# Attention weights divided before they are spread, a residual on TensorE, the first norm on two engines, and one rank per step

## The chip, the core and the metric

The kernel runs on one core of one Trainium2 chip. The core has a matrix engine (TensorE, PE in the profile; its weight loads are the row PEld), a vector engine (VectorE, DVE), a scalar engine (ScalarE, ACT), GpSimd (POOL) and SyncE (SP), which here only issues transfers. Each works through its own list of instructions in order, and waits on semaphores for the others. Matmul results go to eight PSUM banks of 128 x 512 fp32; everything else lies in SBUF. The metric is the device time of one launch in microseconds (us): less is better.

## What is computed

One transformer block over 2048 positions of width 512, in bf16: x plus local attention of the normalised x, then that plus a gated MLP of its normalised self. Attention has 32 heads of 16; each position attends to 8 earlier ones, 0, 2, ..., 14 back.

```python
def _A_ref(x, wqkv, wo):                     # H = 32, Dh = 16, W = 8, dil = 2
    qkv = (x @ wqkv).reshape(B, S, 3, H, Dh).transpose(2, 0, 3, 1, 4)
    q, k, v = qkv[0], qkv[1], qkv[2]
    ...
    logits = jnp.einsum("bhsd,bhswd->bhsw", q, kg) * scale
    logits = jnp.where(mask[None, None, :, :], logits, -1e9)
    attn = _softmax(logits, axis=-1)
    o = jnp.einsum("bhsw,bhswd->bhsd", attn, vg)
    return o.transpose(0, 2, 1, 3).reshape(B, S, D) @ wo

def _B_ref(x, W_gate, W_up, W_down):         # W_gate, W_up: 512 x 1376
    gate, up = x @ W_gate, x @ W_up
    gate = gate * (gate > 0)
    return (gate * up) @ W_down

h = x + _A_ref(_layernorm(x), A_wqkv, A_wo)
return h + _B_ref(_layernorm(h), B_W_gate, B_W_up, B_W_down)
```

## The kernel before

The positions are cut into four chunks of 512, each into four blocks of 128 rows. The x rows stay in SBUF as `x_sm` and are overwritten by h. Each chunk goes through the same stages:

- First norm (`layernorm` without a residual): mean and variance of a block on DVE (L429, L432), 1/sqrt as Ln and Exp on ACT (L442, L446), the normalised rows (L487 on DVE for chunk 0, L484 on ACT for the others), four PE transposes of a block against the identity (L494), and a copy of two blocks at once out of PSUM (L512 on ACT; L510 on DVE for the second pair of chunk 0).
- q, k and v, transposed: twelve groups of four matmuls (L544), each copied out of PSUM by ACT (L552). In chunk 0 the first two groups are made in two halves of 256 positions.
- Scores: DVE multiplies q with four shifted views of k at once (L591, 128 x 4096; four of them in a chunk), PE sums over the 16 dimensions of a head with the 0/1 matrix `sel` (L597), ACT takes the exponential (L606). Chunk 0 multiplies the first 16 columns with a mask (L609).
- Spreading: each weight is copied over the 16 dimensions of its head by the 0/1 matrix `spread` (L625), and ACT copies the eight results to SBUF (L632). The sums of the weights come from the same matrix (L639); ACT makes 1/sum as exp(-ln) (L642, L645).
- Values: DVE multiplies the spread weights with eight shifted views of v (L662, four in a chunk), adds the eight in three steps (L665), and multiplies the result by 1/sum (L669).
- Output: four groups of four matmuls (L700); DVE adds x and takes the row sum at the same time (L705).
- Second norm: a small DVE step for the mean (L414), squares with a sum on ACT (L420), Ln and Exp (L439, L446), rows on DVE (L487), transposes and copies as above.
- MLP: 11 tiles of up and gate, 8 matmuls each (L727), copied by ACT (L731, and L734 with Relu), multiplied by DVE (L747); then for each block 11 matmuls (L759), an addition of h on DVE (L763) and a store from SP (L766).

The order is not the order of the loops. `add` records each step with an engine, an estimated length, what it depends on, and the buffers that it takes and uses. `Plan.order` then runs a list schedule: among the steps of an engine that could start within a small window (`LOOK`) of the earliest, it takes the one with the smallest `prio`, and gives it buffers from small pools: eight PSUM banks for all uses, five big buffers of 128 x 4096, three for exponentials, one for 1/sum. The order found is the order in which instructions are issued. `prio` comes from the table `PRIO`, one number for each kind of step and chunk, shared by all steps of that kind.

`setup` comes before all: it issues the loads (two for the x rows of chunk 0, one on SP and one on ACT), loads the ACT table, makes the constant matrices, and 54 small matmuls keep PE busy until the first rows are ready (`NWARM`, L522).

Of the kernel before, what the change touches and what calls it, by code (L numbers as in the profile page):

```python
# [8 lines left out]
P = 128  # L9
# [8 lines left out]
PRIO = {  # L18
    "warm": (329, 0, 0, 0),
    "xst": (-357, -495, 2394, -54),  # L20
    "xag": (-520, -862, -182, 1996),
    "xrl": (-362, -296, 194, 2166),
    "xre": (-82, 283, 2306, 886),
    "xxn": (-286, 2378, 367, 2013),
    "xtp": (540, 1594, 641, 716),
    "xte": (-646, 2834, 2727, 2443),
    "qkh0": (442, 0, 0, 0),
    "qkv0": (418, 417, 1697, 353),
    "qe0": (1262, 2340, 2135, 2291),
    "qkh1": (1644, 0, 0, 0),  # L30
    "qkv1": (449, 1372, 2578, 2742),
    "qe1": (2915, 2429, 2602, -366),
    "qkv2": (352, 2556, 1012, 1671),
    "qe2": (2725, 402, 863, 106),
    "qkv3": (453, 1501, 226, 815),
    "qe3": (2462, 2595, 2528, 2174),
    "qkv4": (1443, 695, 1687, 267),
    "qe4": (-122, 2839, 177, 2325),
    "qkv5": (701, 873, 594, 1878),
    "qe5": (-44, -211, -170, 2493),  # L40
    "qkv6": (862, 1457, 638, 395),
    "qe6": (-199, -327, 2260, -230),
    "qkv7": (487, 427, 68, 358),
    "qe7": (402, 2319, 2485, -311),
    "qkv8": (1720, 1667, 1519, 453),
    "qe8": (2802, 2488, 2656, 114),
    "qkv9": (1851, -242, 2722, 391),
    "qe9": (1309, 2749, 876, 2302),
    "qkv10": (1764, 857, 1851, 1678),
    "qe10": (2412, 1400, 2395, 458),  # L50
    "qkv11": (2427, 1522, 1794, 722),
    "qe11": (2598, 2825, -204, 2326),
    "pr0": (-482, 1697, -427, 2119),
    "sc0": (1698, 2659, 1551, 1498),
    "ex0": (2396, 2052, 1825, -25),
    "mk0": (2108, 0, 0, 0),
    "pr1": (-469, 1768, -500, 2606),
    "sc1": (404, 855, 418, 1193),
    "ex1": (1517, 142, -363, 143),
    "mk1": (-591, 0, 0, 0),  # L60
    "bc0": (1924, 469, 3082, 309),
    "be0": (-60, -227, 44, 2335),
    "bc1": (-281, 491, 1693, 187),
    "be1": (-373, 324, 2173, 119),
    "den": (1891, 635, 1806, 811),
    "dl": (2476, 2727, -37, 2595),
    "dr": (2494, 2236, 2409, 3002),
    "mu0": (-490, -741, -300, -559),
    "tree0": (-169, -269, -240, -508),
    "om0": (1670, 1359, 1810, -68),  # L70
    "mu1": (-422, -682, -366, -477),
    "tree1": (-140, -329, -243, -384),
    "om1": (-229, -267, 2395, -350),
    "mu2": (-555, -491, 2098, -268),
    "tree2": (-170, 1809, -660, 904),
    "om2": (-521, 1855, -320, -517),
    "mu3": (-551, 1681, 1796, 1815),
    "tree3": (-437, 1819, -540, 1964),
    "om3": (1672, 1855, -287, 2080),
    "wo0": (627, 1946, 489, 2577),  # L80
    "rs0": (-246, -458, -830, -312),
    "wo1": (438, 583, 385, 3140),
    "rs1": (-643, 2078, 1855, 2067),
    "wo2": (313, 69, 182, 553),
    "rs2": (-732, -369, -32, 1663),
    "wo3": (1166, 959, 49, 924),
    "rs3": (-414, -240, 1839, -148),
    "hnm": (-209, -423, 2603, -326),
    "hsq": (2388, 2706, 2324, -39),
    "hrl": (-604, -445, 2636, -334),  # L90
    "hre": (2395, -231, 2261, 2466),
    "hxn": (-412, -519, -293, -471),
    "htp": (609, 1635, 1868, 152),
    "hte": (1320, 2163, 155, 494),
    "mm0": (1484, 427, 528, 389),
    "ue0": (-673, 2837, 2251, 2336),
    "ge0": (44, 2326, -675, 97),
    "gu0": (2058, -433, -474, -124),
    "mm1": (823, 1820, 930, -289),
    "ue1": (1892, 191, 2067, -310),  # L100
    "ge1": (2639, 225, 2423, 2049),
    "gu1": (-496, -252, 1690, -742),
    "mm2": (-16, 412, 2609, 908),
    "ue2": (2776, 2713, -363, 2679),
    "ge2": (-65, 2678, 2266, 2262),
    "gu2": (2019, -373, -285, 1530),
    "mm3": (1801, -279, -278, 2624),
    "ue3": (2151, 164, 2100, 2147),
    "ge3": (-79, 2604, 224, -393),
    "gu3": (-491, -577, -568, 1516),  # L110
    "mm4": (471, 1194, -255, 2655),
    "ue4": (109, 43, 210, 2788),
    "ge4": (2240, 2269, 103, 3043),
    "gu4": (-304, -564, 2366, -656),
    "mm5": (88, 1884, 2524, 706),
    "ue5": (121, -114, 1286, 1403),
    "ge5": (-228, 2600, -52, 2852),
    "gu5": (-362, -366, 1055, 1556),
    "dn0": (415, 2726, 1868, 1679),
    "o0": (-185, 2463, -169, 1484),  # L120
    "os0": (-1500, -1424, -1612, -1426),
    "dn1": (438, 584, 2860, -448),
    "o1": (-495, -599, 1809, 1682),
    "os1": (-1609, -1383, -1616, -1425),
    "dn2": (1621, 2632, 1892, 368),
    "o2": (1891, -170, 2256, 1030),
    "os2": (-1268, -1189, -1208, -1424),
    "dn3": (2453, 2779, 469, 3112),
    "o3": (2772, 2257, -622, -485),
    "os3": (-1239, -1323, -1444, -1438),  # L130
    "xnb": (0, -605, -729, -589),
}
# [35 lines left out]
class Plan:  # L168
# [9 lines left out]
    def add(self, key, *a, **k):  # L178
        op = Op(*a, **k)
        op.key = key  # L180
        if key and key[0] in PRIO:
            op.prio = PRIO[key[0]][key[1]]
        op.seq = len(self.ops)
        self.ops.append(op)
        for b in set(op.take) | set(op.use):
            b.left += 1
        return op
# [57 lines left out]
def kernel(  # L245
# [18 lines left out]
    W = 8  # L264
# [26 lines left out]
    spread = sb.tile([P, P], BF16, name="spread")  # L291
    mask = sb.tile([P, 2, PADL], BF16, name="mask")
# [37 lines left out]
    sel_i, sp_i, mk_i = ints[:, 0:H], ints[:, H:H + P], ints[:, H + P:H + P + PADL]  # L330

    def setup():

        w3_r = A_wqkv.rearrange("(dt p) f -> p dt f", p=P)
        nc.sync.dma_start(x_sm[:, 0:2, :], x_rows[:, 0:2, :])
        nc.scalar.dma_start(x_sm[:, 2:4, :], x_rows[:, 2:4, :])
        for c, q in enumerate((nc.sync, nc.scalar, nc.sync)):
            q.dma_start(w3_sb[c][:], w3_r[:, :, c * D:(c + 1) * D])
        nc.sync.dma_start(x_sm[:, BPC:2 * BPC, :], x_rows[:, BPC:2 * BPC, :])
# [4 lines left out]
        for tk in range(2, NCK):  # L344
            nc.sync.dma_start(x_sm[:, tk * BPC:(tk + 1) * BPC, :], x_rows[:, tk * BPC:(tk + 1) * BPC, :])
# [11 lines left out]
        nc.gpsimd.iota(sp_i[:], pattern=[[1, H], [0, DQ]], base=0, channel_multiplier=0)  # L357
        nc.gpsimd.iota(mk_i[:], pattern=[[1, PADL]], base=0, channel_multiplier=0)
# [10 lines left out]
        V.tensor_scalar(out=spread[:], in0=sp_i[:], scalar1=cf[:, 1:2], scalar2=None, op0=ALU.is_equal)  # L369
        for hf in range(2):  # L370
            V.tensor_scalar(out=mask[:, hf, :], in0=mk_i[:], scalar1=cf[:, 2 + hf:3 + hf],
                            scalar2=None, op0=ALU.is_ge)
# [7 lines left out]
    NWARM = 54  # L380
    DMAT = ()

# [11 lines left out]
    xload = [None] * NCK  # L394
    for tk in range(NCK):
        xload[tk] = add(None, "LD", 0.0, None, lat=[3.3, 11.0, 22.0, 24.0][tk])
    wload = {n: add(None, "LD", 0.0, None, lat=v) for n, v in
             (("q", 5.7), ("k", 7.0), ("v", 8.5), ("o", 12.5), ("u", 16.5), ("g", 20.5), ("d", 28.0))}

    def layernorm(tk, src, dst_slots, pr, groups, on_act, residual=None):  # L400
# [7 lines left out]
        for grp in groups:  # L408
            ag, xns = [], {}
            lo, hi = grp[0], grp[-1] + 1  # L410
            for j in grp:
                if residual:
# [6 lines left out]
                    def f_sq(j=j, xn=xns[j]):  # L419
                        nc.scalar.activation(out=xn.t[:], in_=x_sm[:, tk * BPC + j, :], func=ACT.Square,  # L420
                                             bias=mv.t[:, j, 0:1], scale=1.0, accum_out=sq.t[:, j:j + 1])

                    a = add((ln + "nm", tk), "DVE", DSM, f_nm, [src[j]], pr, take=[mv], use=[sm], lat=DL)
                    ag.append(add((ln + "sq", tk), "ACT", AX + 0.2, f_sq, [a], pr, take=[sq, xns[j]], use=[mv], lat=AL))
                else:
# [8 lines left out]
                    a = add((ln + "st", tk), "DVE", DST, f_st, [src[j]], pr, take=[st], lat=DL)  # L434
                    ag.append(add((ln + "ag", tk), "DVE", DSM, f_ag, [a], pr, take=[mv], use=[st], lat=DL))

            def f_ln(lo=lo, hi=hi):
# [3 lines left out]
                else:  # L441
                    nc.scalar.activation(out=rs.t[:, lo:hi], in_=mv.t[:, lo:hi, 1], func=ACT.Ln,  # L442
                                         bias=eps_t[:, 0:1], scale=1.0)
# [10 lines left out]
            l = add((ln + "rl", tk), "ACT", AS, f_ln, ag, pr, take=[rs], use=[sq or mv], lat=AL)  # L454
            e = add((ln + "re", tk), "ACT", AS, f_ex, [l], pr, use=[rs], lat=AL)
            if on_act:
                e = add((ln + "nb", tk), "DVE", DSM, f_nb, [e], pr, take=[nb], use=[mv, rs], lat=DL)
# [69 lines left out]
    for tk in range(NCK):  # L527
# [49 lines left out]
        for hf in range(2):  # L577
# [38 lines left out]
            exd.append(a)  # L616


        ab, abd = Buf(big_s), []
        for hf in range(2):  # L620
            bcs = [Buf(at_s) for _ in range(4)]

# [195 lines left out]
```

## Time and profile before

| what | value |
|---|---|
| median of 8 runs | 211.1 us (211.01 to 212.92) |
| the profiled execution: its time, its span | 211.13 us, 209.3 us |
| PE busy, matmuls | 198.0 us (95%), 1122 |
| DVE busy, instructions | 169.4 us (81%), 253 |
| ACT busy, instructions | 137.7 us (66%), 262 |
| first q matmul | 9.54 us |
| first gate/up matmul | 74.31 us |
| last matmul ends | 205.89 us |
| chain of waits, by engine | PE 69%, DVE 24%, issue 3%, ACT 2%, DMA 2% |
| granted TensorE clock | 0.997 |

The span is what the profiler saw of the core, from the first to the last instruction; the time of a run is longer by what lies around it. The chain of waits is followed back from the last instruction: at each step to what released it, or to the instruction before it on its engine. In rows of the timeline the brackets give the idle time of the engine ahead of a group and what ended it.

### The profile page before, as it was taken

How to read it: one execution, taken by the hardware profiler on the slowest of the kernel's cores; microseconds unless marked ns; L12 is line 12 of the kernel's file. 1: busy time of each engine (PE TensorE's matmuls, PEld its weight loads, DVE VectorE, ACT ScalarE, POOL GpSimd, SP SyncE). 2: the span in 40 equal slices, each digit the busy share in tenths (PEclk: the TensorE clock that was granted, in tenths of full speed). 3: DMA queues.
4: the chain of work that ended last, by engine and by line, in shares of the span. 5: the costliest groups of instructions: out<-in, count | busy, mean ns of one | idle time of the engine just before them, and what ended most of it. 6: DMA issues, size and time to landing. Idle time of an engine off the chain costs nothing.

```text
span 209.3 us, 2967 instructions
## 1 busy us (share of the span) xinstructions
PE 198.0 (95%) x1122; PEld 96.7 (46%) x1142; DVE 169.4 (81%) x253; ACT 137.7 (66%) x262; POOL 1.6 (1%) x13
## 2 busy tenths in 40 slices
PE   8799899999998789999999999999999999999993
PEld 8664345544543344444454444444444445444441
DVE  5799999999998999999999999859999972122024
ACT  2369999979798887449776643677654644666210
POOL 3000000000000000000000000000000000000000
PEclk9999999999999999999999999999999999999998
DMA  6999800000000000000000000000000002000003
GB/s 203 366 401 375 266 7 2 0 0 0 3 0 0 0 3 0 0 0 3 0 27 25 0 30 0 8 17 28 0 25 0 25 28 75 0 0 2 3 21 105
DMA packets 8638, 10.71 MB, mean 51 GB/s; under 512 B 464, under 2 KB 7472, under 8 KB 8624
## 3 DMA queue, kind: packets, MB, share of 16 engines
q1 hardware_dynamic: 7824, 9.73, 13.4%
q10 hardware_dynamic: 800, 0.79, 1.1%
q8 instruction: 9, 0.15, 0.3%
q14 instruction: 5, 0.04, 0.1%
HBM read 8.42 MB, written 2.10 MB: 50 GB/s over the span
## 4 chain that ended last, share of the span: by engine, by line
PE 69%; DVE 24%; issue 3%; ACT 2%; DMA 2%; DVEq 0%; ACTq 0%
PE bank L727 36%; PE bank L759 18%; DVE big L591 8%; PE bank L700 5%; PE bank L544 5%; DVE big L665 4%; DVE big L662 4%; DVE st L429 3%; PE bank L494 2%; PE bank L597 2%; DMA x_sm<-in_A_x_dram 2%; DVE x_sm L705 1%; ACT quad L512 1%; DVE row L487 1%; DVE mv L432 1%
## 5 line engine op out<-in xcount | busy, mean ns | idle before, releaser
L727 PE MATMUL bank<-quad,wu_sb 128*128 128x512 bf16 (+1 forms) x173 | 44.9, 379 | 0.2
L727 PE MATMUL bank<-quad,wg_sb 128*128 128x512 bf16 (+1 forms) x173 | 44.7, 379 | 0.1
L759 PE MATMUL bank<-wd_sb,gT 128*128 128x512 bf16 (+1 forms) x170 | 39.7, 379 | 0.4 <-issue 0.2
L731 ACT CAST up_sb<-bank 128x512 bf16<-128x512 f32 (+1 forms) x44 | 25.6, 586 | 18.8 <-PE bank L727 12.2
L665 DVE TENSOR_TENSOR big<-big 128x2048 bf16<-128x2048 bf16 (+2 forms) x48 | 37.0, 777 | 1.0
L734 ACT ACTIVATE gr<-bank 128x512 bf16<-128x512 f32 (+1 forms) x44 | 26.1, 600 | 16.0 <-PE bank L727 13.1
L591 DVE TENSOR_TENSOR big<-quad,kT 128x4096 bf16<-128x4096 bf16 x16 | 36.0, 2284 | 0.7 <-ACT kT L552 0.7
L662 DVE TENSOR_TENSOR big<-big,vT 128x4096 bf16<-128x4096 bf16 x16 | 36.3, 2284 | 0.0
L747 DVE TENSOR_TENSOR gT<-gr,up_sb 128x1024 bf16<-128x1024 bf16 (+1 forms) x24 | 15.2, 641 | 25.6 <-ACT gr L734 25.4
L727 PEld LDWEIGHTS <-wu_sb 128*128 128x128 bf16 (+1 forms) x176 | 17.5, 100 | 20.8 <-issue 0.8
L727 PEld LDWEIGHTS <-wg_sb 128*128 128x128 bf16 (+1 forms) x176 | 17.6, 100 | 20.4
L759 PEld LDWEIGHTS <-gT 128*128 128x128 bf16 (+1 forms) x176 | 16.7, 98 | 20.2 <-issue 1.3
L632 ACT CAST big<-bank 128x512 bf16<-128x512 f32 x32 | 16.6, 627 | 2.3 <-PE bank L625 2.3
L512 ACT COPY quad<-bank 128x1024 bf16<-128x1024 bf16 x15 | 14.8, 1033 | 5.0 <-PE bank L494 5.0
L544 PE MATMUL bank<-quad,wv_sb 128*128 128x512 bf16 x61 | 15.7, 380 | 1.1 <-ACT quad L512 0.8
L544 PE MATMUL bank<-quad,wq_sb 128*128 128x512 bf16 (+1 forms) x65 | 15.5, 366 | 0.8 <-ACT quad L512 0.6
L544 PE MATMUL bank<-quad,wk_sb 128*128 128x512 bf16 (+1 forms) x67 | 15.5, 367 | 0.1
L420 ACT ACTIVATE row<-x_sm,mv 128x512 bf16<-128x512 bf16 x16 | 11.5, 733 | 5.3 <-DVE mv L414 5.3
L700 PE MATMUL bank<-wo_sb,quad 128*128 128x512 bf16 x63 | 14.6, 379 | 0.4 <-DVE quad L669 0.4
L763 DVE TENSOR_TENSOR row<-x_sm,bank 128x512 bf16<-128x512 bf16 x16 | 10.8, 684 | 4.7 <-PE bank L759 3.2
L429 DVE BATCH_NORM_STATS2 st<-x_sm 128x6 f32<-128x512 bf16 x16 | 10.5, 670 | 1.9 <-DMA x_sm<-in_A_x_dram 1.9
L597 PE MATMUL bank<-big,sel 128*32 128x512 bf16 x128 | 9.7, 384 | 2.5 <-DVE big L591 2.5
(55 smaller groups left out, 158.5 us busy)
## 6 DMA issues: line engine op xcount, KB each, us to landing
out_dram<-row SPq DMA_DIRECT2D x16, 128.0 KB, 1.7
x_sm<-in_A_x_dram SPq DMA_DIRECT2D x3, 512.0 KB, 15.1
wu_sb<-in_B_W_up_dram SPq DMA_DIRECT2D x1, 1376.0 KB, 13.2
wg_sb<-in_B_W_gate_dram SPq DMA_DIRECT2D x1, 1376.0 KB, 15.9
wd_sb<-in_B_W_down_dram SPq DMA_DIRECT2D x1, 1280.0 KB, 17.4
wq_sb<-in_A_wqkv_dram SPq DMA_DIRECT2D x1, 512.0 KB, 6.3
wk_sb<-in_A_wqkv_dram ACTq DMA_DIRECT2D x1, 512.0 KB, 7.0
wv_sb<-in_A_wqkv_dram SPq DMA_DIRECT2D x1, 512.0 KB, 7.5
```

What stands on the lines that cost most here:

```text
L429: V.bn_stats(out=st.t[:], in_=x_sm[:, tk * BPC + j, :])
L512: nc.scalar.copy(out=o, in_=i)
L544: nc.tensor.matmul(mm.t[:, lo:hi], lhsT=w3_sb[c][:, dt, t:D:NT], rhs=xnT.t[:, dt, lo:hi], start=(dt == 0), stop=(dt == NT - 1))
L591: V.tensor_tensor(out=pb.t[:].rearrange("p (t w) s -> p t w s", t=2), in0=q4, in1=k4, op=ALU.mult)
L632: nc.scalar.copy(out=ab.t[:, w, :], in_=bc.t[:])
L662: V.tensor_tensor(out=mt.t[:], in0=ab.t[:], in1=v8, op=ALU.mult)
L665: V.tensor_tensor(out=mt.t[:, 0:n, :], in0=mt.t[:, 0:n, :], in1=mt.t[:, n:2 * n, :], op=ALU.add)
L700: nc.tensor.matmul(od.t[:], lhsT=OT.t[:, t, j * P:(j + 1) * P], rhs=wo_sb[:, t, :], start=(t == 0), stop=(t == NT - 1))
L727: nc.tensor.matmul(mm.t[:fs, :], lhsT=w_sb[:, dt, ft * P: ft * P + fs], rhs=hnT.t[:, dt, :], start=(dt == 0), stop=(dt == NT - 1))
L731: nc.scalar.copy(out=ub.t[:fs, i, :], in_=um.t[:fs, :])
L734: nc.scalar.activation(out=gr.t[:fs, i, :], in_=gm.t[:fs, :], func=ACT.Relu)
L759: nc.tensor.matmul(od.t[:], lhsT=gts[ft].t[:fs, ft % 2, j * P:(j + 1) * P], rhs=wd_sb[:fs, ft, :], start=(ft == 0), stop=(ft == NFT - 1))
```

## The change

Six edits, of which the last replaces the whole table of priorities.

1. In chunks 1 to 3 (`EARLY`) the exponentials are multiplied by 1/sum before they are spread: two multiplications of 128 x 512 on DVE (`am0`, `am1`) instead of four after the sums of the values (`om`). A new 0/1 matrix `same` gives the sum of the weights in the layout of the exponentials. The last of the three additions writes the attention output directly.
2. In chunk 0 (`RPE`) the residual is a fifth matmul into the bank of the output group, against the identity. ACT copies the bank to `x_sm` and takes the row sum, and the squares of the second norm are taken from the bank.
3. The rows of chunk 0 are loaded block by block, two on SP and two on ACT. Blocks 0 and 1 are one group of the norm, block 2 and block 3 one each; the statistics of block 3 are two passes on ACT. Each block is copied out of PSUM by itself, blocks 1 and 3 by DVE. Four groups of q and k, not two, are made in halves.
4. The x rows of chunks 2 and 3 are loaded ahead of the weights of the output and of the MLP.
5. The last block of chunk 3 is finished in two halves of 256 columns: matmuls, addition, store.
6. `PRIO` gives way to `RANK`, 753 numbers, one for each call of `add`. Some estimated lengths and landing times change, and `NWARM` goes from 54 to 48.

`OPE` and `MERGE` are empty and `BCN` is 4, so the branches that they guard make no change.

```diff
+RANK = [
+    4, 1, 5, 2, 0, 3, 47, 6, 7, 29, 171, 229, 201, 272, 727, 10, 12, 8, 11, 14,
...
-        if key and key[0] in PRIO:
-            op.prio = PRIO[key[0]][key[1]]
+        if RANK:
+            op.prio = RANK[op.seq]
...
-        nc.sync.dma_start(x_sm[:, 0:2, :], x_rows[:, 0:2, :])
-        nc.scalar.dma_start(x_sm[:, 2:4, :], x_rows[:, 2:4, :])
+        for j in range(BPC):
+            (nc.scalar if j % 2 else nc.sync).dma_start(x_sm[:, j:j + 1, :], x_rows[:, j:j + 1, :])
...
-        nc.sync.dma_start(x_sm[:, BPC:2 * BPC, :], x_rows[:, BPC:2 * BPC, :])
+        for tk in range(1, NCK):
+            nc.sync.dma_start(x_sm[:, tk * BPC:(tk + 1) * BPC, :], x_rows[:, tk * BPC:(tk + 1) * BPC, :])
...
+        nc.gpsimd.iota(sm_i, pattern=[[0, 4], [1, H]], base=0, channel_multiplier=0)
+        V.tensor_scalar(out=same[:], in0=sm_i, scalar1=cf[:, 1:2], scalar2=None, op0=ALU.is_equal)
...
-    NWARM = 54
+    NWARM = 48
+    EARLY = (1, 2, 3)
+    RPE, OPE = (0,), ()
...
+                elif tk == 0 and j == BPC - 1:
+                    def f_su(j=j, xn=xns[j], sm=sm):
+                        nc.scalar.activation(out=xn.t[:], in_=x_sm[:, j, :], func=ACT.Copy,
+                                             accum_out=sm.t[:, j:j + 1])
...
+                        nc.scalar.activation(out=xn.t[:], in_=x_sm[:, j, :], func=ACT.Square,
+                                             bias=mv.t[:, j, 0:1], scale=-1.0, accum_out=mv.t[:, j, 1:2])
...
-        groups = [[0, 1], [2, 3]] if tk == 0 else [[0, 1, 2, 3]]
+        groups = [[0, 1], [2], [3]] if tk == 0 else [[0, 1, 2, 3]]
...
-                nc.tensor.matmul(dn.t[:], lhsT=spread[:], rhs=exs[hf].t[:], start=(hf == 0), stop=(hf == 1))
+                nc.tensor.matmul(dn.t[:], lhsT=(same if tk in EARLY else spread)[:], rhs=exs[hf].t[:], start=(hf == 0), stop=(hf == 1))
...
+        if tk in EARLY:
+            for hf in range(2):
+                def f_am(ex=exs[hf], rc=rc):
+                    V.tensor_tensor(out=ex.t[:], in0=ex.t[:], in1=rc.t[:], op=ALU.mult)
+
+                exd[hf] = add(("am%d" % hf, tk), "DVE", D2, f_am, [rcd], apr + 1, use=[exs[hf], rc], lat=DL)
...
+            if tk not in EARLY:
+                oev[t] = add(("om%d" % t, tk), "DVE", D2, f_om, [m, rcd], tpr, take=[OT], use=[mt, rc], lat=DL)
...
+                if tk in RPE:
+                    nc.tensor.matmul(od.t[:], lhsT=identity[:], rhs=x_sm[:, tk * BPC + j, :],
+                                     start=False, stop=True)
...
+                if tk in RPE:
+                    nc.scalar.activation(out=r, in_=od.t[:], func=ACT.Copy, accum_out=sm.t[:, j:j + 1])
...
+        parts = [(j, 0, D) for j in range(BPC)]
+        if tk == NCK - 1:
+            parts[-1:] = [(BPC - 1, 0, D // 2), (BPC - 1, D // 2, D)]
+        for n, (j, c0, c1) in enumerate(parts):
...
```

## The prediction

> **What bounds it now.** I read the time in slices first, then the chain of waits, then the order of instructions around the place where the chain changes engine.
>
> ```profile
> PE   8799899999998789999999999999999999999993
> DVE  5799999999998999999999999859999972122024
> ```
>
> Each digit is a fortieth of the span, 5.2 us. TensorE (PE) is full almost everywhere; VectorE (DVE) is equally full until four fifths of the span. Which of them sets the pace is told by the chain:
>
> ```profile
> 51.33 2.43 DVE x_sm L705 x8
> 53.76 0.25 DVE mv L414 x4
> 54.01 5.80 DVE big L591 x3
> ...
> 70.13 1.37 DVE row L487 x4
> 71.51 2.21 DVE big L591
> 73.72 0.04 issue
> 73.76 0.61 PE bank L597 x8
> 74.38 0.32 PE bank L727
> ```
>
> Columns are start, length, what. From 23 to 74 us the chain runs almost wholly through DVE; from 74 to 206 us through PE. At 70.13 DVE writes the normalised rows of chunk 0 (L487), and only then can the first gate/up matmul (L727) go. The busy times of the two stretches and of the worst part:
>
> ```profile
> 9.54:74.31 64.77, 59.93 (x402) 29.95 (x408) 62.24 (x80) 56.99 (x110) 0.00 (x0) 1.00 0.26 91
> 74.31:205.90 131.59, 130.78 (x655) 60.10 (x664) 100.12 (x150) 77.38 (x148) 0.00 (x0) 1.00 0.04 14
> ...
> 50.00:74.31 24.31, 21.45 (x165) 9.36 (x165) 23.60 (x26) 20.98 (x43) 0.00 (x0) 1.00 0.00 1
> ```
>
> After length come PE, weight loads, DVE, ACT. After 74.31 PE never stops (the missing 0.8 us are gaps of one matmul between unbroken neighbours). Before, PE loses 4.8 us, 2.9 of them after 50 us, when the q/k/v matmuls run out and DVE still works.
>
> Is a busy PE working at its rate? The Trainium skill warns ("Trainium Kernel Development and Optimization", Best Practices) that matmul busy time is a bad measure of the distance to the roofline. By that rule the 131 us could hide slack. The rows decide: groups of four L727 matmuls start at 109.23, 110.09 and 110.95, 0.216 us per matmul. The page "TensorE: Matmul & The Clock Gate" (Wait — 56ns, not 53.3ns?) gives 215.7 ns for 512 columns warm. The 131 us are work and move only by matmuls added or taken away. **So the end = first L727 start + about 131.6 + tail,** and the change is worth what it does to the start and the tail.
>
> **The parts.** All sums stand against the profiled execution: span 209.3, its own time 211.13, so 1.83 lies around the span; the median of the runs is 211.1, the same.
>
> *Head.* x comes in four loads, not two; three row blocks get their statistics on DVE, the fourth on ACT. Before:
>
> ```profile
> 7.28 1.42 DVE L487 TENSOR_SCALAR row<-x_sm,mv,rs 128x512 bf16<-128x512 bf16 x4
> 9.54 0.60 PE L544 MATMUL bank<-quad,wq_sb 128*128 128x256 bf16 x4 [0.38 <-ACT quad L512]
> ```
>
> Four statistics at 0.80 us each (4.07 to 7.28) precede the rows; then a 1024-wide copy of 1.02 us stands before q. Now three statistics end at 6.5, but xn waits for ACT: sum 0.72 and its read 0.19 (rows of L420), a small DVE step 0.15, square 0.72 and read, and the Ln/Exp of blocks 0 and 1 around it: about 7.0. Rows 0.34 each, transposes 0.35, 512-wide copies 0.6 by L731; the block-1 copy stands behind the other rows on DVE, until 9.05. First q matmul at about 9.1: -0.45. Bounds -0.8 (x lands earlier) and +0.2 (the fourth block lands last). The page "DMA: Bandwidth & Descriptors" (Anatomy of one DMA) prices a transfer at 2.0 us plus bytes/436 GB/s, fitted on another queue: halving 256 KB would save 0.3. The row is 3.3 us with other loads in flight, so I book 0. wq and wk are issued some 0.5 us later (two more issues, 0.43 to 0.51 each): landing 7.5 becomes 8.0, 8.3 becomes 8.8, still before use. x of chunks 2 and 3 now goes ahead of wo, up and gate weights: 1 MB, 2.6 us at 400 GB/s; wo is used at 48.9, the others at 74. The extra matrix `same` costs POOL 0.49 and DVE 0.28 (L357, L369) inside the DVE wait ending at 4.07. Six fewer warm-up matmuls shorten work that ends 0.88 before anything is ready: nothing.
>
> *Residual of chunk 0.* Four identity matmuls: +0.87 on PE. DVE loses 2.43 (the x8 row above); ACT gains four copies with a sum. By the page "ScalarE: Activation LUTs" (What ACT_TABLE_LOAD costs), 186 ns + 0.833 per element less 93 overlap gives 0.52 each, 2.1; it prices no sum. The nearest row, L420 with its sum, is 0.72, so up to 2.9. Either is more than DVE paid; it pays only because ACT is idle 3.3 us in the 24.3 above. I take 2.5.
>
> *Weights divided first.* In chunks 1 to 3 four multiplications per chunk (L669, 0.34 apart) become two. DVE: -4.1 + 2.0 = -2.1 over all. In exchange the spreading (L625) waits for sum 0.5, Ln 0.62, Exp 0.65, two multiplications 0.76 and hops: 2.7 us more latency per chunk. That hides behind other DVE work if the order leaves room. In the rank table the divisions of chunk 1 stand four large operations ahead of its first use in L662; those of chunks 2 and 3 lie among gate/up steps. Behind a late spread, PE holds score and q/k/v matmuls and ACT its copies L632, for which L662 on DVE waits. Exposed cost: 0, bound 2.7 for chunk 1 alone, since later PE has gate/up work.
>
> *Order.* Assigning the ranks to steps in the order of their `add` calls, DVE has 13 products L591 ahead of the normalised rows of chunk 0, not 12, and two divisions. Up to their end at 71.50: -2.43 (residual), +2.20 (product), +0.7 (divisions), -0.4 (statistics queued in fours, 0.69 a block where singles take 0.80; bounds 0 and -0.8), -0.7 (the wait for a key copy before 67.92: the keys of chunk 3 are ranked earlier; bounds 0 and -1.1). Sum -0.6: end at 70.9, bounds 70.1 and 72.0. From there 1.85 (71.50 to 73.35: transposes and copy) to the first L727: **72.8**, not 74.3. Could PE follow? Its work to that point: 59.9 + 0.87 + 0.55 (one score group more) - 0.33 (one spread less) = 61.0, from 9.1: 70.1 to 70.5 with small gaps. So PE still waits for DVE, 2.3 us.
>
> *Behind 72.8.* 131.6 - 0.55 + 0.33 = 131.4. DVE had 91.6 us from 71.5 to its last chunk-3 sum at 163.1; less 2.7 and one product less it ends near 157.6, well before PE needs it: no new stop. PE ends at 204.2.
>
> *Tail.* Now 3.4 us from the last matmul: L763 0.69, then the store. The last block is cut in halves: the half addition should take 0.36 (0.61 pitch, mostly per element); the half store saves 0.15 by the DMA page's rate, nothing if 1.7 is all latency. Tail 3.0, bounds 2.9 and 3.4. Twice as many weight loads (98 ns) still fit beside 256-column matmuls (0.109).
>
> Span 207.2; with 1.83: **209.0 us**, 1.0% less.
>
> **Rivals.** (a) *PE becomes the bound:* the DVE waits fall away and L727 starts at 70.5. 70.5 + 131.4 + 2.9 = 204.8, time 206.6. For it: DVE has 3 us of slack in its bounds; against it: a thirteenth product stands ahead. (b) *Nothing arrives:* the moved product and a remaining key wait eat the gain; L727 at 74.3, 205.7 + 3.0 = 208.7, time 210.5. For it: DVE's sum without the two estimates is +0.5. (c) *Slower: DVE waits in order for ACT.* The small residual steps (L414) and the chunk-1 division stand in DVE's queue ahead of three products and wait for ACT, which must first copy four residual blocks. DVE has three products, 6.6 us, to cover output matmuls 2.2, ACT copies and Exp 2.8: 5.0. The margin is 1.6. ACT was busy 23.7 of 25 us just before (25 to 50), and the four residual banks stay held until they are squared, so half of PSUM is gone while q/k/v still need copying. Once ACT is more than 1.6 late each us goes to the chain; 4 us gives L727 at 76.8, span 211.2, time 213.0.
>
> **Chances.** Forecast 0.45 (208.2 to 210.0), (a) 0.18, (b) 0.21, (c) 0.16. No change that can be told is within 0.5%, 210.0 to 212.2. Faster: forecast, (a) and a part 0.08 of (b), 0.71; same 0.13; slower 0.16. The range 206.7 to 212.0 leaves 0.06 below and 0.13 above.
>
> **What would show it.** Right: first q matmul near 9.1; L487 of chunk 0 ending near 71; first L727 near 72.8; PE unbroken after it; tail 3.0. Wrong: a DVE wait on ACT between 50 and 70 us, PE waiting for PSUM banks there, or a PE gap after 75 us because a spread came late.

## The result, and the profile after

The changed kernel takes 209.4 us (median; 207.58 to 209.87), the kernel before 211.14 in all the runs made beside it. The ratio is 0.9891, with a 95% interval of 0.9866 to 0.9915: 1.1% faster. The profiled execution took 209.29 us with a span of 207.4. A ratio is taken over the undisturbed executions and not from the two medians, whose quotient here is 0.9918, since 9 of the 32 executions of the kernel before took 212.1 to 212.9 us.

The time in slices (a digit is a fortieth of the span in tenths) of the changed kernel:

```profile
PE   8598999999999999999999999999999999999994
DVE  6559999999999999999879998659999564011414
```

The hole of PE around the fourteenth slice (before: 8, 7, 8) is gone; a new one stands at the start, a 5 on PE and two on DVE, from 5 to 16 us. The chain of waits (start, length, what) says where the path runs:

```profile
2.66 9.91 DMA x_sm<-in_A_x_dram
12.59 2.47 DVE st L390 x4
...
69.65 0.91 PE bank L456 x10
70.56 2.21 DVE big L549
72.77 0.04 issue
72.82 0.61 PE bank L555 x8
73.43 0.32 PE bank L721
```

It now begins with the loads. The rows of chunk 1 are issued at 2.66 and DVE starts on them at 12.59. The normalised rows of chunk 0 end at 70.56, and a score group (L555), which waits for a product, still stands in PE's queue ahead of the first gate/up matmul (L721). The same lines in the timeline of the first microseconds, with the idle time ahead in brackets:

```profile
9.49 1.50 PE L502 MATMUL bank<-quad,wq_sb 128*128 128x256 bf16 x12 [1.41 <-DMA wq_sb<-in_A_wqkv_dram]
12.59 1.88 DVE L390 BATCH_NORM_STATS2 st<-x_sm 128x6 f32<-128x512 bf16 x3 [4.30 <-DMA x_sm<-in_A_x_dram]
```

PE waits 1.41 us for wq and DVE 4.30 us for x of chunk 1, which in the kernel before it had at 10.67. What DVE makes of its time from there to the end of the rows, in windows (length, then PE, weight loads, DVE, ACT); first the kernel before, then the changed one:

```profile
10.67:71.50 60.83, 56.92 (x369) 28.34 (x374) 59.08 (x78) 54.18 (x106) 0.00 (x0) 1.00 0.25 89
```

```profile
12.59:70.56 57.97, 55.63 (x364) 27.01 (x369) 57.83 (x73) 53.22 (x108) 0.00 (x0) 1.00 0.25 90
```

DVE's idle time falls from 1.75 to 0.14 us, its busy time by 1.25. The stretch is 2.86 us shorter, and it starts 1.92 later: 0.94 is left, which is what the first L721 gains (74.31 to 73.36). The 1.9 us of the span are this 0.95, then 0.39 from there to the last matmul (131.58 to 131.19), and 0.55 in the tail (3.4 to 2.85).

### The profile page after: what moved, and what is told of

Read it like the earlier page. It is cut to its first block, busy times and chain, and to the rows that moved or that the text cites. A ratio compares the mean times of both kernels' runs of the same rounds, so it can differ in the third digit from the quotient of the medians.

```text
span 207.4 us, 2992 instructions
## 1 busy us (share of the span) xinstructions
PE 197.8 (95%) x1139; PEld 97.8 (47%) x1159; DVE 162.4 (78%) x241; ACT 140.5 (68%) x277; POOL 1.8 (1%) x14
## 4 chain that ended last, share of the span: by engine, by line
PE 64%; DVE 20%; issue 5%; DMA 5%; ACT 4%; SPq 1%; DVEq 0%
PE bank L721 37%; PE bank L758 18%; DVE big L549 7%; PE bank L683 5%; DMA x_sm<-in_A_x_dram 5%; DVE big L637 4%; DVE big L640 4%; DVE st L390 3%; ACT big L622 2%; PE bank L456 2%; ACT row L422 1%; PE bank L555 1%; ACT quad L510 1%; DVE quad L644 1%; PE bank L616 1%
## 5 line engine op out<-in xcount | busy, mean ns | idle before, releaser
L721 PE MATMUL bank<-quad,wu_sb 128*128 128x512 bf16 (+1 forms) x176 | 41.8, 379 | 0.1
L721 PE MATMUL bank<-quad,wg_sb 128*128 128x512 bf16 (+1 forms) x169 | 41.4, 379 | 0.3
L758 PE MATMUL bank<-wd_sb,gT 128*128 128x512 bf16 (+3 forms) x183 | 40.2, 366 | 0.2
L640 DVE TENSOR_TENSOR big<-big 128x2048 bf16<-128x2048 bf16 (+2 forms) x36 | 30.6, 890 | 0.1
L721 PEld LDWEIGHTS <-wu_sb 128*128 128x128 bf16 (+1 forms) x176 | 17.5, 100 | 20.7 <-issue 0.8
L721 PEld LDWEIGHTS <-wg_sb 128*128 128x128 bf16 (+1 forms) x176 | 17.5, 100 | 20.6 <-issue 0.4
L758 PEld LDWEIGHTS <-gT 128*128 128x128 bf16 (+1 forms) x187 | 17.8, 98 | 19.0 <-issue 0.9
L769 DVE TENSOR_TENSOR row<-x_sm,bank 128x512 bf16<-128x512 bf16 (+1 forms) x17 | 10.8, 652 | 9.5 <-PE bank L758 8.9
L470 ACT COPY quad<-bank 128x1024 bf16<-128x1024 bf16 (+1 forms) x16 | 15.2, 967 | 4.2 <-PE bank L456 3.9
L683 PE MATMUL bank<-wo_sb,quad 128*128 128x512 bf16 x62 | 15.0, 379 | 0.1
L360 ACT ACTIVATE row<-x_sm,mv 128x512 bf16<-128x512 bf16 x12 | 8.6, 718 | 8.1 <-DVE mv L352 7.8
L390 DVE BATCH_NORM_STATS2 st<-x_sm 128x6 f32<-128x512 bf16 x15 | 9.5, 680 | 4.6 <-DMA x_sm<-in_A_x_dram 4.6
L456 PE MATMUL bank<-identity,row 128*128 128x128 bf16 x128 | 10.2, 220 | 2.4 <-DVE row L425 1.4
```

Of the source, the lines that this page charges most:

```text
L390: V.bn_stats(out=st.t[:], in_=x_sm[:, tk * BPC + j, :])
L470: nc.scalar.copy(out=o, in_=i)
L640: V.tensor_tensor(out=mt.t[:, 0:n, :], in0=mt.t[:, 0:n, :], in1=mt.t[:, n:2 * n, :], op=ALU.add)
L683: nc.tensor.matmul(od.t[:], lhsT=OT.t[:, t, j * P:(j + 1) * P], rhs=wo_sb[:, t, :], start=(t == 0), stop=(t == NT - 1 and tk not in RPE))
L721: nc.tensor.matmul(mm.t[:fs, :], lhsT=w_sb[:, dt, ft * P: ft * P + fs], rhs=hnT.t[:, dt, :], start=(dt == 0), stop=(dt == NT - 1))
L758: nc.tensor.matmul(od.t[:, c0:c1], lhsT=gts[ft].t[:fs, ft % 2, j * P:(j + 1) * P], rhs=wd_sb[:fs, ft, c0:c1], start=(ft == 0), stop=(ft == ...
```

## The experiments

Two theories. **A:** the first L721 comes a fixed length of DVE work after x of chunk 1 has landed; four small loads put that landing late, and an earlier landing or a shorter stretch moves the time one for one. **B:** something else takes over (PE, ACT, the issue times of the loads), so that this is swallowed. Each text says what they make of its run. Times are medians with their extremes, ratios are to the kernel before. All edits are to the changed kernel; where steps fall away, so do their ranks, and where new ones come they stand beside the steps that they belong to.

**Two loads for chunk 0, as before.**

```diff
-        for j in range(BPC):
-            (nc.scalar if j % 2 else nc.sync).dma_start(x_sm[:, j:j + 1, :], x_rows[:, j:j + 1, :])
+        nc.sync.dma_start(x_sm[:, 0:2, :], x_rows[:, 0:2, :])
+        nc.scalar.dma_start(x_sm[:, 2:4, :], x_rows[:, 2:4, :])
```

> The changed kernel with the four x loads of chunk 0 put back to two of 256 KB; all else the same, the order too. Theory A (the four loads open the hole of 152 GB/s between 4 and 5 us, and with it make wq land at 9.4 and x of chunk 1 at 12.6): the hole closes, wq lands by 8.2, x of chunk 1 by 11.0, the first L721 starts at 71.5 to 72.3 instead of 73.4, time 207.4 to 208.3 us. Theory B (the loads are late for another reason, or DVE's start does not matter because PE is the limit): landing or first L721 stay within 0.4 us, time 209.0 to 209.8.

Measured: 207.3 us (207.18 to 207.83), 0.9797 [0.9759, 0.9835]. The timeline of this kernel:

```profile
8.69 1.47 PE L502 MATMUL bank<-quad,wq_sb 128*128 128x256 bf16 x12
10.47 1.88 DVE L390 BATCH_NORM_STATS2 st<-x_sm 128x6 f32<-128x512 bf16 x3 [1.60 <-DMA x_sm<-in_A_x_dram]
```

x of chunk 1 lands 2.1 us sooner, and L721 starts at 71.25, also 2.1 sooner: the stretch has 60.78 us here and 60.77 in the changed kernel. A holds. The windows of 1 us show what differs in the transfers (the last column is GB/s, the one before it the busy share of the 16 DMA engines); first the changed kernel, then this one:

```profile
3.00:4.00 1.00, 1.00 (x12) 1.00 (x11) 0.67 (x3) 0.42 (x1) 0.00 (x0) 1.00 0.99 270
4.00:5.00 1.00, 1.00 (x15) 1.00 (x13) 1.00 (x4) 0.64 (x2) 0.00 (x0) 1.00 0.57 152
5.00:6.00 1.00, 0.57 (x11) 0.40 (x8) 0.88 (x4) 0.96 (x4) 0.00 (x0) 1.00 0.82 249
```

```profile
3.00:4.00 1.00, 1.00 (x12) 1.00 (x11) 0.19 (x2) 0.06 (x1) 0.00 (x0) 1.00 1.09 369
4.00:5.00 1.00, 1.00 (x12) 1.00 (x10) 0.90 (x2) 0.53 (x1) 0.00 (x0) 1.00 1.08 376
5.00:6.00 1.00, 1.00 (x13) 1.00 (x10) 1.00 (x5) 0.49 (x4) 0.00 (x0) 1.00 0.97 323
```

With four loads of 128 KB the DMA engines run half empty between 4 and 5 us in this profile. Over these three windows 671 KB are moved (GB/s over 1 us each, added), with two loads of 256 KB 1068 KB. The 397 KB left are about 1.1 us at 360 GB/s; the landings of wq (9.44 against 6.7) and of x (12.59 against 10.47) are later by more. How deep the hole is varies: the three profiles below that also have the four loads in front show 173, 236 and 300 GB/s from 4 to 5 us, with DVE's start on chunk 1 at 12.56, 13.07 and 11.89. The six profiles with two loads and nothing else moved (the kernel before among them) show 370 to 387 GB/s and 10.45 to 10.67. The two groups don't overlap, so that four loads in front make x late is shown; but within the first group the landing doesn't follow the rate of this one window, so the hole is not the whole of the reason.

**Wq issued late, but two loads.** To part the number of loads from the later issue, each queue gets a load of 8 KB into a spare tile (`late`) between x and its weights:

```diff
+        nc.sync.dma_start(late[0][:], x_rows[:, 0:1, 0:32])
+        nc.scalar.dma_start(late[1][:], x_rows[:, 2:3, 0:32])
```

> Two x loads as in the first experiment, and on each of the two queues a load of 64 bytes per partition into a spare tile between x and wq or wk, so that wq and wk are issued as late as with four loads and behind as many loads, while x is not cut smaller. Theory A (wq and wk behind two loads each, and so issued 0.4 later: the engines run dry before their data flow): the hole comes back, under 250 GB/s for most of 4 to 6 us; x of chunk 1 lands at 11.5 to 13, time 208.3 to 209.6. Theory B (the hole comes from the cut of x into 128 KB loads): no hole, x of chunk 1 lands by 11.0, time 207.2 to 207.8.

Measured: 208.22 us (207.84 to 209.05), 0.9835 [0.9797, 0.9872]: between the two. x of chunk 1 lands at 11.27, 0.8 of the 2.1 us, at 270 GB/s between 4 and 5 us; L721 follows at 72.04, again 60.77 later. So about 0.8 us go with the later issue and the 8 KB load that makes it; the rest goes with the cut of x into loads of 128 KB ahead of the weights, and by what mechanism stays open. The split is rough: it rests on one profile, and the profiles with four loads differ by 1.2 us among themselves.

**Small loads interleaved with the weights** (SP: block 0, wq, block 2, wv; ACT: block 1, wk, block 3).

```diff
-        for j in range(BPC):
+        for j in range(2):
             (nc.scalar if j % 2 else nc.sync).dma_start(x_sm[:, j:j + 1, :], x_rows[:, j:j + 1, :])
-        for c, q in enumerate((nc.sync, nc.scalar, nc.sync)):
+        for c, q in enumerate((nc.sync, nc.scalar)):
             q.dma_start(w3_sb[c][:], w3_r[:, :, c * D:(c + 1) * D])
+        for j in range(2, BPC):
+            (nc.scalar if j % 2 else nc.sync).dma_start(x_sm[:, j:j + 1, :], x_rows[:, j:j + 1, :])
+        nc.sync.dma_start(w3_sb[2][:], w3_r[:, :, 2 * D:3 * D])
```

> The changed kernel with its four x loads, but wq on SP and wk on ACT are issued behind the first x load of each queue, not the second; wv and the rest behind. Theory A (the hole is the gap between small x loads and a late wq): the engines stay above 300 GB/s between 4 and 6 us, wq lands by 7.6, x of chunk 1 by 11.2, and the time is 207.3 to 208.5, with blocks 2 and 3 of x later than before. Theory B (many small loads starve the engines wherever they stand): the hole stays, x of chunk 1 lands after 12.0, time 209 or more.

Measured: 211.1 us (210.1 to 211.88), 0.996 [0.9933, 0.9987]. The hole is gone (386 GB/s from 4 to 5 us, wq there at 6.1, x of chunk 1 at 10.65), so B is out: four small loads don't starve the engines when wq and wk stand between them and are issued at 1.2 us, as with two loads. But A's time was missed by about 3 us. The timeline shows two reasons:

```profile
8.04 0.63 ACT L375 ACTIVATE row<-x_sm 128x512 bf16<-128x512 bf16 x1 [4.49 <-DMA x_sm<-in_A_x_dram]
8.58 0.19 ACT L375 ACTIVATION_READ_ACCUMULATOR row<-x_sm 128x1 f32 x1
8.80 0.15 DVE L379 TENSOR_SCALAR mv<-sm 128x1 f32<-128x1 f32 x1 [3.73 <-ACT row L375]
9.93 1.38 DVE L428 TENSOR_SCALAR row<-x_sm,mv,rs 128x512 bf16<-128x512 bf16 x4 [0.16 <-ACT rs L410]
10.40 1.89 PE L459 MATMUL bank<-identity,row 128*128 128x128 bf16 x16 [4.13 <-DVE row L428]
```

Block 3, behind 512 KB of weights, reaches ACT at 8.04. On DVE the small step L379 waits for it, ahead of the rows of all four blocks: the rows start at 9.93, with two loads at 6.83. A wait for one block of four holds all four, because it stands first in an ordered queue. The second reason is the clock: PE stood still for 4.13 us, and from about 9.5 to 16.3 us the granted clock is 0.50, so that the twelve q matmuls that take 1.47 us with two loads take 2.74 here. The first product of chunk 1 starts at 19.00 instead of 14.97. Of these 4.0 us 3.1 are the later rows and the rest, about 0.9, goes with the slower matmuls; no run here has the one without the other.

**The residual of chunk 0 back on DVE.**

```diff
-    RPE, OPE = (0,), ()
+    RPE, OPE = (), ()
```

> The changed kernel with the residual of chunk 0 put back on DVE (no identity matmuls, squares read from x_sm), same ranks. Theory A (DVE's sum up to the normalised rows of chunk 0 sets the start of L721): DVE gets 2.4 us of additions back in that stretch, PE loses 0.87 of work; L721 starts 1.5 to 2.4 later, time 210.9 to 211.8. Theory B (PE's own work is the limit there): L721 starts 0.5 to 0.9 earlier, time 208.5 to 208.9. Theory C (ACT's copies are what DVE waits for): L721 within 0.5, time 209.0 to 209.9.

Measured: 212.34 us (210.23 to 213.89), ratio 1.0015 [0.999, 1.004], as the kernel before; by the ratios 0.012 of 211 or 2.6 us more than the changed kernel. A holds, a little above its ranges. x of chunk 1 lands at 12.56, as in the changed kernel, and L721 starts at 75.84, 2.5 later. On DVE's timeline the additions are back ahead of the rows:

```profile
65.24 0.68 DVE L694 SCALAR_TENSOR_TENSOR x_sm<-x_sm,bank 128x512 bf16<-128x512 bf16 x1
65.85 0.09 DVE L694 DVE_READ_ACCUMULATOR x_sm<-x_sm,bank 128x1 f32 x1
...
71.66 1.38 DVE L425 TENSOR_SCALAR row<-x_sm,mv,rs 128x512 bf16<-128x512 bf16 x4
```

**The division late again.**

```diff
-    EARLY = (1, 2, 3)
+    EARLY = ()
```

> The changed kernel with chunks 1 to 3 dividing after the sums of the values again (twelve multiplications instead of six); ranks kept, each of the twelve is ranked right behind its last addition. Theory A (DVE's sum up to the normalised rows sets the start of L721, and later DVE has slack): the two divisions of chunk 1 leave that stretch, L721 starts 0.4 to 0.8 earlier, 3.4 us more DVE work afterwards is hidden, time 208.5 to 209.1. Theory B (the early division is where the gain came from, because DVE is close to the limit until 163 us): PE stops before the output matmuls of chunks 1 to 3, time 210.5 to 212.5.

Measured: 208.91 us (207.9 to 209.46), 0.9864 [0.9822, 0.9906]; the stretch from landing to L721 is 60.13 us instead of 60.77, so the two divisions that stood ahead of L721 cost 0.65. But from L721 to the last matmul PE needs 131.6 us instead of 131.2: 0.44 of the gain is lost again there, and B is right to that extent. The medians cannot part this run from the changed kernel; the places in the trace can. Here q begins at half the granted clock:

```profile
9.87 2.75 PE L502 MATMUL bank<-quad,wq_sb 128*128 128x256 bf16 x12 [1.91 <-DMA wq_sb<-in_A_wqkv_dram]
```

**Two loads and the late division.**

> Two x loads as in the first experiment, and chunks 1 to 3 divide after the sums of the values. Theory A (DVE's sum up to the normalised rows sets the start of L721; the early division costs two multiplications there and its saving later is hidden): L721 starts 0.3 to 0.7 before the 71.3 of the first experiment, time 206.6 to 207.1. Theory B (the early division is worth its place once the loads are on time): 207.6 to 208.5.

Measured: 207.15 us (206.96 to 207.8), 0.9801 [0.9765, 0.9837]. L721 starts at 70.69, 0.56 before that of the two loads alone, as A had it; but the gain in time, 0.15 us, can't be told from none. The traces say where it goes. PE between 154 and 161 us, with two loads alone and then with the late division as well:

```profile
155.55 1.03 PE L721 MATMUL bank<-quad,wg_sb 128*128 128x512 bf16 x4
156.41 1.03 PE L721 MATMUL bank<-quad,wu_sb 128*128 128x512 bf16 x4
157.28 2.75 PE L721 MATMUL bank<-quad,wg_sb 128*128 128x512 bf16 x12
159.87 1.03 PE L683 MATMUL bank<-wo_sb,quad 128*128 128x512 bf16 x4
```

```profile
154.98 1.03 PE L721 MATMUL bank<-quad,wg_sb 128*128 128x512 bf16 x4
156.11 1.02 PE L721 MATMUL bank<-quad,wu_sb 128*128 128x512 bf16 x4
156.97 2.94 PE L721 MATMUL bank<-quad,wg_sb 128*128 128x512 bf16 x12
159.74 1.03 PE L683 MATMUL bank<-wo_sb,quad 128*128 128x512 bf16 x4
```

From the first of these groups to L683 PE takes 4.32 us with the early division and 4.76 with the late one, so the last matmul ends only 0.12 us sooner. DVE, with six multiplications more in all, comes to its addition L769 at 158.15, 1.8 us later behind L721 than with the early division. That PE waits there for a bank which DVE or ACT frees late is likely, but not shown by itself.

**The last block in one piece**, once with four loads and once with two (in the second, the first edit above as well).

```diff
-        if tk == NCK - 1:
+        if False:
             parts[-1:] = [(BPC - 1, 0, D // 2), (BPC - 1, D // 2, D)]
```

> The changed kernel with the last block finished in one piece. All theories: the tail from the last matmul to the end of the span grows from 2.85 back to 3.3 to 3.5, time 209.8 to 210.1. If the split cost PE something by its double weight loads, PE's end comes earlier by that and the time is nearer to 209.5.

> Two x loads, and the last block in one piece. All theories: the tail grows from 2.85 to 3.3 to 3.5 and the time from 207.3 to 207.7 to 208.0, with less scatter than in the run with four loads. If the halves cost PE time, the gain is less.

Measured: 209.5 us (208.29 to 210.04), 0.9891 [0.9845, 0.9937], with four loads; 207.7 (207.65 to 208.36), 0.9827 [0.9794, 0.9859], with two. The first is the time of the changed kernel: its x landed at 11.89 in the profile instead of 12.59, and that spread covers the effect. The second is 0.4 above the two loads alone. PE ends alike, at 202.45 and 202.44, so halves cost it nothing; the chain of waits ends on the whole addition:

```profile
202.47 0.69 DVE row L769
```

where the half takes 0.42. The tail is 3.46 us here and 2.96 there.

**The first norm as before**, two loads: blocks 2 and 3 one group, all statistics on DVE, copies of two blocks. Four groups of q and k are still made in halves.

```diff
-                elif tk == 0 and j == BPC - 1:
+                elif False:
...
-        groups = [[0, 1], [2], [3]] if tk == 0 else [[0, 1, 2, 3]]
+        groups = [[0, 1], [2, 3]] if tk == 0 else [[0, 1, 2, 3]]
...
-            step = 1 if tk == 0 and not residual else 2
+            step = 2
```

> Two x loads, and the first norm of chunk 0 as before: four statistics on DVE, two groups, copies of two blocks. Theory A (DVE's chain starts when x of chunk 1 lands, whatever the head does): q starts 0.7 to 0.9 later than the 8.7 of the first experiment, L721 within 0.3 of 71.3, time 207.1 to 207.7. Theory B (a later head is a later end): 208.0 to 208.3.

Measured: 207.96 us (207.55 to 208.76), 0.9835 [0.98, 0.9869]. q starts at 9.06 instead of 8.69 and L721 at 71.50 instead of 71.25. The trace speaks for a small worth of this part, at most 0.25 us, of which 0.1 is a later landing (10.57 against 10.47); the median, 0.66 up, lies between the two expectations and decides nothing.

**The order and the load order alone:** the work of the kernel before (late division, no residual on PE, old norm, whole last block, two loads) under the new ranks; what is left of the other edits is that four groups of q and k are made in halves, `same` and the 48 warm-up matmuls.

> The work of the kernel before (late division, residual on DVE, first norm all on DVE, one piece at the end, two x loads), in the new order, with the new order of the loads of x and weights. Each step has the rank of its counterpart. Theory A (the gain is DVE work taken out of the stretch before L721): against the first experiment DVE has 2.4 of residual more and 0.7 of divisions less, so L721 starts near 73.0, and the tail is 3.4: time 209.4 to 210.4. Theory B (the ranks are the gain, the other edits little): 207.5 to 208.5. Theory C (the ranks are made for the other edits and are bad for the old work): 211.5 or more.

Measured: 210.55 us (210.14 to 212.93), 0.9965 [0.9932, 0.9997]; A's upper end was 210.4. One rank per step, with the order of the loads, is worth about a third of a per cent without the rest; the interval ends just short of no change. DVE's stretch to the end of the rows is 61.06 us, against 60.83 before, though it has a product of 2.20 more in it. (In this profile the granted clock is 0.50 from about 9.2 to 12.5 us and again from about 70 to 77, so its L721 is not compared.)

**What follows from all this:** two loads, the late division, and x of chunk 1 issued ahead of wv, which is not used before q and k are made.

```diff
-        for c, q in enumerate((nc.sync, nc.scalar, nc.sync)):
+        for c, q in enumerate((nc.sync, nc.scalar)):
             q.dma_start(w3_sb[c][:], w3_r[:, :, c * D:(c + 1) * D])
-        for tk in range(1, NCK):
+        nc.sync.dma_start(x_sm[:, BPC:2 * BPC, :], x_rows[:, BPC:2 * BPC, :])
+        nc.sync.dma_start(w3_sb[2][:], w3_r[:, :, 2 * D:3 * D])
+        for tk in range(2, NCK):
```

> Two x loads, late division in chunks 1 to 3, and x of chunk 1 loaded ahead of wv. Theory A (with the loads on time PE has 1.0 us of idle time left between the first q matmul and L721, so an earlier DVE can win that much at most): x of chunk 1 lands near 9.2, L721 starts at 70.2 to 70.7, time 206.5 to 207.1. Theory B (DVE's start still carries to the end): L721 near 69.4, time 205.7 to 206.2.

Measured: 206.47 us (206.33 to 207.7), 0.9759 [0.972, 0.9798], the fastest median of all and clear of the changed kernel's interval, though not of that of the two loads alone. DVE starts on chunk 1 at 8.85, and L721 comes at 69.73, between the two forecasts. The window from the first q matmul to the first gate/up matmul (L723 in this version):

```profile
8.58:69.73 61.15, 60.93 (x424) 31.02 (x425) 60.33 (x73) 57.63 (x115) 0.00 (x0) 1.00 0.29 102
```

PE is busy for all but 0.22 of 61.15 us. DVE has nothing more to give here: the next gain in this stretch would have to take matmuls away. Behind it PE needs 131.6 us, with the 0.44 of the late division in it; dividing late in chunk 1 alone might save both, but was not tried.

## Why the prediction was right, and which of its steps were not

The time came within 0.4 us of the forecast, through errors that cancelled: that it came so close is in part luck.

| step | predicted | changed kernel | two loads |
|---|---|---|---|
| first q matmul | 9.1 | 9.49 | 8.69 |
| DVE starts on chunk 1 | 10.67, unquestioned | 12.59 | 10.47 |
| rows of chunk 0 end | 70.9 | 70.56 | 68.45 |
| from there to the first L721 | 1.85 | 2.80 | 2.80 |
| first L721 | 72.8 | 73.36 | 71.25 |
| to the last matmul | 131.4 | 131.19 | 131.19 |
| tail | 3.0 | 2.85 | 2.96 |
| span | 207.2 | 207.4 | 205.4 |

**Head: the step that failed.** What it booked for the compute was too much: the rows start at 6.25 and not at 7.0, since the first statistics start at 3.52 instead of 4.07 (an earlier x was booked as 0) and the rest is a little quicker; with two loads, where the rows start at 6.83, q follows at 8.69, before the 9.1 of the forecast. The split of the norm is worth 0.37 of that. What failed is "wq and wk are issued some 0.5 us later ...: landing 7.5 becomes 8.0, 8.3 becomes 8.8, still before use". Wq landed at 9.44, and x of chunk 1, queued behind, 1.9 us late; I never asked for that one, though DVE's stretch begins with it. A shift of the issue was booked as an equal shift of the landing; the windows show that the engines moved less as well.

**"Sum -0.6".** DVE's stretch shrank by 2.86. The residual was booked at -2.43, and undoing it measures 2.5; the divisions at +0.7, measured 0.65; the thirteenth product at +2.20 is there. Statistics gave some -0.7 for -0.4, waits -1.6 for -0.7. One term was not in the sum: the twelve additions of chunk 0 (L640), which the old order did one chain after another and the new one takes in turn over four chains. On DVE's timeline, the kernel before and then the changed one:

```profile
44.53 3.47 DVE L665 TENSOR_TENSOR big<-big 128x1024 bf16<-128x1024 bf16 x5
```

```profile
51.04 4.63 DVE L640 TENSOR_TENSOR big<-big 128x1024 bf16<-128x1024 bf16 x8
```

Singles of the three widths are about 1.21, 0.69 and 0.42 us long. The five before (one wide, two middle, two narrow) add up to 3.45, about the whole group. The eight after (one, four and three) add up to 5.2 but take 4.63: they overlap, by some 0.08 each. Before, a step that needs the result of the one just ahead starts only when that has ended: a middle addition holds DVE for 0.73 us from start to start, after the change for 0.60; a wide one for 1.25 and 1.14. Start to start, the twelve took 9.44 us before and take 8.29 now: -1.15. With the new ranks on the old work they take 8.29 too, so it is the order that does it. That and the waits made -2.86 out of -0.6, and the late landing took back 1.92.

**"From there 1.85".** Too short by 0.95, and the chain I had quoted showed it: 71.51 to 74.38 by way of a product and its score group, 2.87. I took the copy of the transposes as the last thing; the score group stood in PE's queue ahead of L727, then as now.

**Behind L721 and the tail** the sums held (0.2 and 0.15 off). PE was not stopped by a late spread. What the early division saves DVE behind L721 was booked as worth nothing there; against the late division it is worth 0.44 us of PE's time, which nearly pays for the 0.65 ahead of L721. The four residual copies on ACT take 0.6 us each from start to start, 2.4 in all for 2.5 booked.

**The rivals.** (a), PE as the bound, did not come in the changed kernel, but it is where the work ends: its 206.6 us is close to what the last version reaches, by other edits, with 206.5. (b), nothing arrives: the key wait it counted on fell away. (c), DVE waiting for ACT: DVE is idle 0.14 us in its whole stretch. PE's order and ACT's copies left room, though ACT was busy for 23.28 of the 24.31 us from 50 to 74.31.

Open: why the loads behind four small ones lag by more than the issue explains, and what sets the clock down in some executions.

## What to carry to other kernels

When loads are split, follow every load behind them to the instruction that begins the critical stretch, and look at the rate of the first microseconds in narrow windows: an earlier first block was worth less here than the later landing of all that came behind it cost. Take the step between two bounds from the chain itself, with each thing queued ahead of the last instruction, not from what that instruction needs. And where one engine sets the pace, the order among its own instructions is worth money too: chains taken in turn run faster than one after another.

## What the runs showed of the hardware

- Four loads of 128 KB ahead of the weights: 152 to 300 GB/s between 4 and 5 us (four profiles), and x of chunk 1 used from 11.89 to 13.07 us on; two of 256 KB: 370 to 387 GB/s and 10.45 to 10.67 (six profiles). The later landings are longer than the shift of the issue (0.43 us for wq: 2.7 later).
- A DVE addition costs about 0.12 us more, start to start, when the next one needs its result (128 x 1024: 0.73 against 0.60; 128 x 2048: 1.25 against 1.14).
- The granted clock fell to 0.50 between 9.2 and 9.7 us in four profiled executions and stayed there for 3.3 us or more (6.8 in the longest); the longest pause of PE in the microseconds before was 1.04, 1.15, 1.91 and 4.13 us. With the late division (1.91) twelve 256-column matmuls took 2.75 us instead of 1.50. Three others with pauses of 1.41 (the changed kernel), 1.59 and 1.63 us kept 1.00. A pause alone, then, doesn't tell it.
